# Taking the last pass over 64 contraction rows out of each product and running it as four 64-row matmuls per pair

## The chip, the core and the metric

The kernel runs on one core of one Trainium2 chip. The metric is the time of one execution on the device in microseconds (us); lower is better. The kernel before was timed in three runs: median 755.26 us, 754.84 to 755.68 us.

## What is computed

The reference mixes two branches with a gate. Only branch B is touched by the change; its core, with S = 2048 and D = 576, is:

```
a = einsum("bsd,ed->bse", x, dft_hid_re)        # x Wr
b = einsum("bsd,ed->bse", x, dft_hid_im)        # x Wi
y = einsum("ts,bse->bte", dft_seq_re, a) - einsum("ts,bse->bte", dft_seq_im, b)
return g * attention(x) + (1 - g) * y           # g = sigmoid(x . gate_w)
```

The products x Wr and x Wi contract over the 576 hidden columns: four chunks of 128 rows and a rest of 64 rows (`KC = 4`, `REST = 64`).

## The kernel before, in words

**Numbers.** Every fp32 operand is split into a high part (ScalarE copies it to the type fp32r, `hi_of`, line 112) and a low part (VectorE subtracts, `lo_of`, line 115). A product is high x high + high x low + low x high; low x low is dropped.

**One product.** `steps` (line 187) lists the matmuls of one 128-row tile of x with one half (288 columns) of a weight matrix: three for each of the four 128-row chunks, then two for the rest:

```
yield xs[:, 4], rhs(4)
yield xs[:, 9], rhs(4)
```

The 64 rest rows of x lie twice in the 128 partitions (`_rows` and `twice` on the host side), the high part in `xs[:, 4]` and the low part in `xs[:, 9]`. Row 4 of the weights, `hi[:, KC]` in `Wide.split` (line 241), holds the high part in partitions 0 to 63 and the low part in 64 to 127. The first of the two matmuls so adds high x high and high x low at once; the second adds low x high, and low x low with it. That makes 14 matmuls of 128 contraction rows, 128 stationary columns and 288 moving columns for one product (line 123 in the profile, through `run`).

**The order of the work.** The program goes through stages: features of k, k-v sums, q and the gate, the output matrix M and its product, then x Wr (`pairs(wdr, mr)`, line 779), the product with Cr (`sequence`, line 642), x Wi (`pairs(wdi, mi)`, line 782), the product with Ci. In `pairs` (line 542) 16 tiles of x are taken in 8 pairs (`NP = 8`); a pair is the four products of two tiles `i` with two column halves `h`. The six first pairs (`for p in range(NP - 2)`, line 574) do all four, tile by tile (pair 0 half by half), and the last two pairs are written apart (lines 589 to 603). After the second half of a tile its slot, one of three, is loaded with a later tile (`load_next`, line 171, a DMA of 320 KB on SyncE's queue) and an earlier loaded one is split (`split_next`). Each product has a PSUM bank, four to a pair, of eight. `columns` (line 552) reads the two banks of half 0 into the factors `f`, `rest` (line 560) reads all four into sums `tsum` and splits them.

**Who orders the queues.** The order on each engine is written before the run by a planner that replays the program against its own cost model (`schedule_with_timeline_sim=True`). SyncE's queue follows program order up to line 756 and the planner from there on. The planner may also move matmuls of one product ahead of those of another.

**What the change and the steps of the prediction touch:** `Wide.__init__` and `Wide.split` (lines 208 and 228), the loop of the six pairs (lines 574 to 582), `columns` and `rest`, and the two `Wide(...)` of Wr and Wi (lines 723 and 760).

Of the kernel before, what the change touches and what calls it, by code (L numbers as in the profile page):

```python
# [9 lines left out]
R = mybir.dt.float32r  # L10
AF = mybir.ActivationFunctionType
# [3 lines left out]
P = 128  # L15
S, D, H, DH = 2048, 576, 32, 18
NT = S // P
KC = 4
REST = D - KC * P
NG, GW = 5, 126  # L20
HALF = D // 2
CU = 4
NCU = NT // CU
NP = NT // 2
# [23 lines left out]
class Ring:  # L48
# [5 lines left out]
    def next(self):  # L54
# [5 lines left out]
TPAIR = 2 * 7 * HALF * 4  # L60
XD = 2 * D * 4
T_AT = 0
ACC_AT = T_AT + NP * TPAIR
SLOT_AT, SLOT = ACC_AT + NT * D * 4 + 256, 7 * BS * P * 4
# [8 lines left out]
LAY_R = dict(xs=(-256, 4864, 15744), hi=(20864, 9984), lo=(26624, 31232),  # L73
             low=(5, 3, 2, 1), high=(6, 0, 4))
LAY_I = dict(xs=(35840, 40960, 20096), hi=(25216, 14336), lo=(31232, 46080),
             low=(0, 4, 2, 3), high=(1, 5, 6))
# [3 lines left out]
def kernel(  # L80
# [14 lines left out]
    nc = tc.nc  # L95
# [4 lines left out]
    def at(offset, shape, dtype=F, name="t"):  # L100
        count[0] += 1
        t = nc.alloc_sbuf_tensor_at(f"{name}_{count[0]}", list(shape), dtype,
                                    offset=base + offset)
        return t.ap()
# [3 lines left out]
    def bank():  # L108
        return psum.tile([P, 512], F, tag="bank", name="bank")

    def hi_of(dst, src, bias=0.0):
        return nc.scalar.activation(dst, src, AF.Copy, bias=bias)  # L112

    def lo_of(dst, src, hi):
        nc.vector.tensor_tensor(out=dst, in0=src, in1=hi, op=ALU.subtract)  # L115

    def add(dst, a, b, op=ALU.add):
        nc.vector.tensor_tensor(out=dst, in0=a, in1=b, op=op)  # L118

    def run(ps, pairs):  # L120
        pairs = list(pairs)
        for n, (a, b) in enumerate(pairs):
            nc.tensor.matmul(ps, a, b, start=(n == 0), stop=(n == len(pairs) - 1))  # L123
# [47 lines left out]
    def load_next():  # L171
        if order:
            xs, raw = new_xs()
            nc.sync.dma_start(out=raw, in_=xa[order.pop(0)])
            raws.append((xs, raw))

    def split_next():
        if raws:
            xs, raw = raws.pop(0)
            hi_of(xs[:, 0:5], raw)  # L180
            lo_of(xs[:, 5:10], raw, xs[:, 0:5])
            split.append(xs)
# [4 lines left out]
    def steps(xs, rhs):  # L187

        for c in range(KC):
            yield xs[:, c], rhs(c)  # L190
            yield xs[:, c], rhs(5 + c)
            yield xs[:, 5 + c], rhs(c)
        yield xs[:, 4], rhs(4)
        yield xs[:, 9], rhs(4)
# [10 lines left out]
    class Wide:  # L205


        def __init__(self, src, lay, start=SLOT_AT, widths=(HALF, HALF)):
            self.src, self.lay, self.got = src, lay, {}
            self.start, self.widths = start, widths  # L210

        def load(self, h, pieces=1, queues=None):
            n = self.widths[h]
# [14 lines left out]
        def split(self, h, n=1):  # L228

            hi, los, rest = self.got[h]  # L230
            for c, lo, raw in los:
                k = lo.shape[1]
                m = max(k * n // KC, 1)
                for a in range(0, k, k // m):
                    cs = slice(a, a + k // m)
                    hs = slice(c + a, c + a + k // m)
                    hi_of(hi[:, hs], raw[:, cs])
                    lo_of(lo[:, cs], raw[:, cs], hi[:, hs])
                    yield
            hi_of(hi[:, KC], rest)  # L240
            lo_of(hi[64:, KC], rest[64:], hi[64:, KC])
            yield

        def row(self, h, j):
# [60 lines left out]
    xs = [First(), split.pop(0)]  # L305
# [34 lines left out]
    for i in range(2, NT):  # L340
        xs = split.pop(0)
# [56 lines left out]
    for c in range(5):  # L398
        ps = [bank(), bank()]
        passes = FULL if c < KC else FULL[:2]  # L400
        for q in range(NCU):
            t = xg_split.pop(0)
            for k in range(CU):
                s = q * CU + k
                for n, (a, b) in enumerate(passes):
                    for h in range(2):
                        nc.tensor.matmul(ps[h][:, :HALF], t[:, a, k], pk[s][:, b, half(h)],  # L407
                                         start=(s == 0 and n == 0),
                                         stop=(s == NT - 1 and n == len(passes) - 1))
# [132 lines left out]
    def pairs(wd, m):  # L542


        def product(b, i, h, xs):
            run(b[i][h], steps(xs[i], lambda j: wd.row(h, j)))

        def banks():
            b12, b11, b22, b21 = (bank()[:, :HALF] for _ in range(4))
            return (b11, b12), (b21, b22)  # L550

        def columns(p, b):

            t = at(T_AT + p * TPAIR, [P, 2, 7, HALF], R, "f")
            for i in range(2):
                hi_of(t[:, 0, i], b[i][0])
                lo_of(t[:, 1, i], b[i][0], t[:, 0, i])
            return t

        def rest(b, t):  # L560
            (b11, b12), (b21, b22) = b
            s = at(Y_AT, [P, 4, HALF], F, "tsum")
            nc.scalar.activation(s[:, 3], b12, AF.Copy)
            add(s[:, 0], s[:, 3], b11, ALU.subtract)
            add(s[:, 2], b22, s[:, 3], ALU.subtract)
            hi_of(t[:, 0, 2], b22)
            add(s[:, 1], b22, s[:, 0], ALU.subtract)
            add(s[:, 3], s[:, 1], b21, ALU.subtract)
            lo_of(t[:, 1, 2], b22, t[:, 0, 2])
            hi_of(t[:, 0, 3:7], s)  # L570
            lo_of(t[:, 1, 3:7], s, t[:, 0, 3:7])
            factors.append(t)

        for p in range(NP - 2):
            xs = [split.pop(0), split.pop(0)]
            b = banks()
            for i, h in sorted(((0, 0), (0, 1), (1, 0), (1, 1)), key=lambda u: u[not p]):
                product(b, i, h, xs)
                if h == 1:
                    load_next()  # L580
                    split_next()
            rest(b, columns(p, b))
            if p == NP - 4:
                m.load(0)
                m.make(0)
        xs_ring.at, xs_ring.n = [T_AT + NP * TPAIR - XS], 0
        load_next()
        split_next()
        last, p = [], NP - 2
        for k in range(2):  # L590
            xs, b = [split.pop(0), split.pop(0)], banks()
            for i in (0, 1) if k == 0 else (1, 0):
                product(b, i, 0, xs)
            if k == 0:
                split_next()
            last.append((b, xs, columns(p + k, b)))
        m.load(1)
        for b, xs, t in last:
            for i in range(2):
                product(b, i, 1, xs)  # L600
            if t is last[0][2]:
                m.make(1)
            rest(b, t)
# [103 lines left out]
    def transposed(i):  # L707

        xs, _ = new_xs("qs", qs_ring)
        banks = [bank(), bank()]  # L710
        twice = at(T_AT + 36864 + (i % 2) * 512, [P, 2, REST], F, "twice")
        nc.vector.tensor_copy(out=twice,
                              in_=acc[i][:, KC * P:].unsqueeze(1).to_broadcast([P, 2, REST]))
        for c in range(5):
            a = acc[i][:, c * P:(c + 1) * P] if c < KC else twice.rearrange("p a b -> p (a b)")
            nc.tensor.transpose(banks[c // KC][:, (c % KC) * P:(c % KC + 1) * P], a, ident)  # L716
        hi_of(xs[:, 0:4], banks[0])
        lo_of(xs[:, 5:9], banks[0], xs[:, 0:4])
        hi_of(xs[:, 4], banks[1][:, :P])
        lo_of(xs[:, 9], banks[1][:, :P], xs[:, 4])  # L720
        return xs

    wdr = Wide(wr, LAY_R)
    qs = transposed(0)
    for i in range(NT):
        if i + LEAD < NT:
# [30 lines left out]


    mr, mi = Matrix(cr, LAY_R), Matrix(ci, LAY_I)
    wdi = Wide(wi, LAY_I)  # L760

    def late(n):
        if n == NP * NB - 3:
# [75 lines left out]
```

## Time and profile before

| | |
|---|---|
| median of three runs | 755.26 us (754.84 to 755.68) |
| the profiled execution's own time | 754.51 us |
| its span, first to last instruction | 752.8 us |
| mean granted TensorE clock | 0.998 |
| TensorE matmul busy / weight load busy | 738.9 us / 736.3 us |
| VectorE busy / ScalarE busy | 543.1 us / 331.3 us |

The span is what one execution's trace shows; the time around it (1.7 us here) is outside every instruction. "PE" is TensorE's matmuls, "PEld" its weight loads, "DVE" VectorE, "ACT" ScalarE, "SP" SyncE. A matmul's recorded duration is longer than the distance to the next one's start, since matmuls are pipelined; what a matmul costs in a full stream is the distance of the starts.

### The profile page before, as it was taken

The numbers are of one execution on the slowest core, as the hardware profiler recorded it, in microseconds if no ns is written. First come the engines' busy times: TensorE is split into PE (matmuls) and PEld (weight loads), VectorE is DVE, ScalarE is ACT, GpSimd is POOL, SyncE is SP. The second block draws the span as 40 slices with busy tenths as digits, with TensorE's granted clock in tenths as the row PEclk, the third lists the DMA queues.
The fourth block names the chain that finished last, engine by engine and source line by source line (L and its number), as shares of the span: only waits on it lengthen the run. The fifth ranks groups of instructions, "written<-read, shape, count | busy, mean of one in ns | idle before, by whom it ended". The sixth has DMA issues, their size and how long they took to land.

```text
span 752.8 us, 13507 instructions
## 1 busy us (share of the span) xinstructions
PE 738.9 (98%) x5540; PEld 736.3 (98%) x5540; DVE 543.1 (72%) x915; ACT 331.3 (44%) x534; POOL 1.6 (0%) x10
## 2 busy tenths in 40 slices
PE   7999999997999999999999999999999999999998
PEld 7999999987999999999999999999999999999998
DVE  5668853757967228778888787778778887788784
ACT  6777334647546435544322323334554232322321
POOL 0000000000000000000000000000000000000000
PEclk9999999999999999999999999999999999999999
DMA  5334534152104013232323223234322243334331
GB/s 165 89 88 157 186 97 140 54 157 63 53 2 147 1 45 89 88 101 91 108 84 107 90 85 112 84 102 140 90 71 94 103 144 125 135 117 139 120 104 45
DMA packets 31641, 75.55 MB, mean 100 GB/s; under 512 B 3227, under 2 KB 8987, under 8 KB 31579
## 3 DMA queue, kind: packets, MB, share of 16 engines
q1 hardware_dynamic: 31291, 74.27, 30.9%
q8 instruction: 44, 0.72, 0.4%
q10 hardware_dynamic: 288, 0.41, 0.2%
q14 instruction: 18, 0.15, 0.1%
HBM read 68.47 MB, written 4.72 MB: 97 GB/s over the span
## 4 chain that ended last, share of the span: by engine, by line
PE 94%; DMA 3%; DVE 1%; issue 1%; ACT 0%; SPq 0%; ACTq 0%; DVEq 0%
PE bank L660 47%; PE bank L123 37%; PE bank L407 8%; DMA xraw<-in_xa_dram 3%; PE bank L716 1%; PE bank L392 1%; DMA wraw<-in_wr_dram 1%; DVE xs L115 0%; DVE wd L115 0%; SPq L507 0%; ACT xs L112 0%; ACT wd L112 0%; DVE acc L465 0%; DVE qs L115 0%; DVE acc L258 0%
## 5 line engine op out<-in xcount | busy, mean ns | idle before, releaser
L660 PE MATMUL bank<-f,c 128*128 128x288 f32 x2688 | 356.8, 295 | 0.0
L660 PEld LDWEIGHTS bank<-f,c 128*128 128x128 f32 x2688 | 356.6, 188 | 0.0
L123 PE MATMUL bank<-wd,xs 128*128 128x288 f32 (+1 forms) x1792 | 246.5, 299 | 10.1 <-ACT xs L112 5.2
L123 PEld LDWEIGHTS bank<-wd,xs 128*128 128x128 f32 x1792 | 242.5, 191 | 12.2 <-ACT xs L112 5.7
L112 ACT ACTIVATE c<-craw 128x1792 fp32r<-128x1792 f32 (+1 forms) x84 | 121.3, 1448 | 224.5 <-DVE craw L118 183.9
L115 DVE TENSOR_TENSOR c<-craw,c 128x1792 fp32r<-128x1792 f32 (+2 forms) x84 | 141.7, 1690 | 36.3 <-ACT c L112 36.1
L118 DVE TENSOR_TENSOR craw<-craw 128x256 f32<-128x256 f32 (+1 forms) x192 | 96.4, 509 | 51.8 <-DMA craw<-in_cr_dram 24.5
L115 DVE TENSOR_TENSOR xs<-xraw,xs 128x640 fp32r<-128x640 f32 (+1 forms) x65 | 52.5, 810 | 25.9 <-ACT xs L112 24.8
L123 PE MATMUL bank<-mw,qs 128*128 128x288 f32 x448 | 63.3, 298 | 0.6 <-DVE qs L115 0.6
L112 ACT ACTIVATE xs<-xraw 128x640 fp32r<-128x640 f32 x63 | 46.3, 737 | 38.5 <-DMA xraw<-in_xa_dram 38.3
L123 PEld LDWEIGHTS bank<-mw,qs 128*128 128x128 f32 x448 | 60.0, 188 | 0.8 <-DVE qs L115 0.8
L407 PE MATMUL bank<-pk,c 128*128 128x288 f32 x448 | 60.8, 296 | 0.0
L407 PEld LDWEIGHTS bank<-pk,c 128*128 128x128 f32 x448 | 59.8, 188 | 0.0
L118 DVE TENSOR_TENSOR y<-bank,y 128x288 f32<-128x288 f32 x63 | 28.6, 453 | 9.5 <-PE bank L660 8.8
L258 DVE SCALAR_TENSOR_TENSOR acc<-bank,e 128x288 f32<-128x288 f32 x64 | 27.8, 448 | 10.2 <-ACT e L257 10.1
L256 ACT ACTIVATE e<-bank 128x288 f32<-128x288 f32 x64 | 25.6, 401 | 18.0 <-PE bank L123 17.9
L115 DVE TENSOR_TENSOR f<-tsum,f 128x1152 fp32r<-128x1152 f32 x16 | 21.7, 1356 | 13.3 <-ACT f L112 13.3
L257 ACT ACTIVATE e<-e 128x288 f32<-128x288 f32 x64 | 28.0, 439 | 0.9
L735 ACT ACTIVATE acc<-bank,gate 128x288 f32<-128x288 f32 x32 | 16.0, 499 | 27.8 <-PE bank L123 27.5
L112 ACT ACTIVATE f<-bank 128x288 fp32r<-128x288 f32 x48 | 19.2, 401 | 20.2 <-PE bank L123 11.7
L115 DVE TENSOR_TENSOR f<-bank,f 128x288 fp32r<-128x288 f32 x48 | 21.4, 448 | 8.7 <-ACT f L112 8.7
L112 ACT ACTIVATE f<-tsum 128x1152 fp32r<-128x1152 f32 x16 | 18.6, 1163 | 17.4 <-DVE tsum L118 17.4
(67 smaller groups left out, 321.0 us busy)
## 6 DMA issues: line engine op xcount, KB each, us to landing
xraw<-in_xa_dram SPq DMA_DIRECT2D x63, 320.0 KB, 3.0
craw<-in_cr_dram SPq DMA_DIRECT2D x32, 512.0 KB, 3.3
craw<-in_ci_dram SPq DMA_DIRECT2D x32, 512.0 KB, 3.3
craw<-in_xg_dram SPq DMA_DIRECT2D x20, 256.0 KB, 3.2
out_dram<-acc SPq DMA_DIRECT2D x14, 288.0 KB, 3.2
wraw<-in_wv_dram SPq DMA_DIRECT2D x5, 288.0 KB
wraw<-in_wr_dram SPq DMA_DIRECT2D x2, 576.0 KB, 4.0
wraw<-in_wi_dram SPq DMA_DIRECT2D x2, 576.0 KB
```

The source lines that it names most:

```text
L112: return nc.scalar.activation(dst, src, AF.Copy, bias=bias)
L115: nc.vector.tensor_tensor(out=dst, in0=src, in1=hi, op=ALU.subtract)
L118: nc.vector.tensor_tensor(out=dst, in0=a, in1=b, op=op)
L123: nc.tensor.matmul(ps, a, b, start=(n == 0), stop=(n == len(pairs) - 1))
L256: nc.scalar.activation(e, ps, AF.Relu, scale=-1.0)
L257: nc.scalar.activation(e, e, AF.Exp, scale=-1.0)
L258: nc.vector.scalar_tensor_tensor(dst, ps, 0.0, e, op0=ALU.max, op1=ALU.add)
L392: nc.tensor.matmul(kv_of(g), wvt[c][:, a, gs], gts[c][:, :, gs], start=(c == 0 and a == 0 and g % 2 == 0), stop=(c == 4 and a == 1), skip_ ...
L407: nc.tensor.matmul(ps[h][:, :HALF], t[:, a, k], pk[s][:, b, half(h)], start=(s == 0 and n == 0), stop=(s == NT - 1 and n == len(passes) - 1))
L660: nc.tensor.matmul(ps[q], c[x][:, l, k], factors[p][:, y, f], start=(p == 0 and i == 0), stop=(p == NP - 1 and i == 2))
L716: nc.tensor.transpose(banks[c // KC][:, (c % KC) * P:(c % KC + 1) * P], a, ident)
L735: nc.scalar.activation(acc[i][:, half(h)], ps[:, :HALF], AF.Copy, scale=gate[:, i:i + 1])
```

## The change

It applies to the six first pairs of the Wr stage and of the Wi stage. The second of the two rest matmuls is taken out of each product. Instead the low rest `xs[i][:, 9]` of each tile is copied by ScalarE into a small buffer of its own (`ends`, four buffers of 512 bytes per partition in a ring, `lows`), and after the four products of a pair four matmuls of 64 contraction rows follow: for half 0 on partitions 0 to 63, for half 1 on 64 to 127. For this the weights' row 4 of half 1 is stored the other way round (`flip`: low part in 0 to 63, high part in 64 to 127). All four banks of a pair are so complete only at its end. Low x low of the rest is no longer added there. Everything else stays.

```diff
-            lo_of(hi[64:, KC], rest[64:], hi[64:, KC])
+            side = slice(0, REST) if self.flip and h == 1 else slice(REST, P)
+            lo_of(hi[side, KC], rest[side], hi[side, KC])
...
+        lows = Ring(T_AT + (NP - 1) * TPAIR, P * 4, 4)
         for p in range(NP - 2):
             xs = [split.pop(0), split.pop(0)]
-            b = banks()
+            b, ends = banks(), []
             for i, h in sorted(((0, 0), (0, 1), (1, 0), (1, 1)), key=lambda u: u[not p]):
-                product(b, i, h, xs)
+                if h == 0:
+                    ends.append(at(lows.next(), [P, P], R, "low"))
+                    nc.scalar.activation(ends[i], xs[i][:, 9], AF.Copy)
+                for n, (a, w) in enumerate(list(steps(xs[i], lambda j: wd.row(h, j)))[:-1]):
+                    nc.tensor.matmul(b[i][h], a, w, start=(n == 0), stop=False)
                 if h == 1:
                     load_next()
                     split_next()
+
+            for i in range(2):
+                for h in range(2):
+                    rows = slice(h * REST, (h + 1) * REST)
+                    nc.tensor.matmul(b[i][h], ends[i][rows], wd.row(h, KC)[rows],
+                                     start=False, stop=True)
             rest(b, columns(p, b))
...
-    wdr = Wide(wr, LAY_R)
+    wdr = Wide(wr, LAY_R, flip=True)
...
-    wdi = Wide(wi, LAY_I)
+    wdi = Wide(wi, LAY_I, flip=True)
```

## Rows read from the trace of the kernel before

**Rows 1.** The page: busy time of each engine, and the granted clock in 40 slices.

```profile
PE 738.9 (98%) x5540; PEld 736.3 (98%) x5540; DVE 543.1 (72%) x915; ACT 331.3 (44%) x534; POOL 1.6 (0%) x10
...
PEclk9999999999999999999999999999999999999999
```

**Rows 2.** The chain that ended last, in time: start us, length us, what, count.

```profile
267.01 66.76 PE bank L123 x504
...
512.04 59.34 PE bank L123 x448
```

**Rows 3.** What TensorE waited for in the whole run: us, times, longest us.

```profile
PE bank L123 <- ACT xs L112: 5.2, 2, 4.0
PE bank L123 <- DVE xs L115: 4.1, 2, 3.8
```

**Rows 4.** Groups with shapes apart, 274.4 to 333.7 us (Wr stage).

```profile
L123 PE MATMUL bank<-wd,xs 128*128 128x288 f32 x448 | 59.5, 295 | 0.0
...
L115 DVE TENSOR_TENSOR f<-bank,f 128x288 fp32r<-128x288 f32 x23 | 10.3, 449 | 8.5 <-ACT f L112 8.5
L115 DVE TENSOR_TENSOR xs<-xraw,xs 128x640 fp32r<-128x640 f32 x12 | 9.8, 820 | 2.6 <-ACT xs L112 2.5
...
L112 ACT ACTIVATE xs<-xraw 128x640 fp32r<-128x640 f32 x12 | 8.8, 737 | 4.9 <-DMA xraw<-in_xa_dram 4.9
L115 DVE TENSOR_TENSOR f<-tsum,f 128x1152 fp32r<-128x1152 f32 x6 | 8.1, 1358 | 7.4 <-ACT f L112 7.4
...
L118 DVE TENSOR_TENSOR tsum<-bank,tsum 128x288 f32<-128x288 f32 x14 | 6.3, 450 | 0.0
L118 DVE TENSOR_TENSOR tsum<-tsum,bank 128x288 f32<-128x288 f32 x14 | 6.2, 446 | 0.6 <-ACT tsum L563 0.6
...
L563 ACT ACTIVATE tsum<-bank 128x288 f32<-128x288 f32 x7 | 2.8, 406 | 2.6 <-DVE f L115 2.0 <-PE bank L123 0.6
```

**Rows 5.** Busy time by stretch: Wr stage, Wi stage, four pairs of each.

```profile
274.40:333.70 59.30, 59.30 (x450) 59.30 (x449) 41.41 (x76) 29.59 (x51) 0.00 (x0) 1.00 0.29 85
512.00:571.30 59.30, 59.30 (x450) 59.30 (x449) 45.95 (x83) 29.51 (x52) 0.00 (x0) 1.00 0.32 95
...
281.70:311.40 29.70, 29.70 (x227) 29.70 (x226) 22.37 (x40) 16.29 (x29) 0.00 (x0) 1.00 0.32 96
519.40:549.10 29.70, 29.70 (x227) 29.70 (x226) 22.43 (x39) 16.86 (x29) 0.00 (x0) 1.00 0.34 98
```

**Rows 6.** Timeline, where stationaries of 72 columns are followed by 128 columns.

```profile
87.74 0.14 PEld L392 LDWEIGHTS bank<-gt,plain 128*72 128x72 f32 x1
87.80 0.19 PEld L407 LDWEIGHTS bank<-pk,c 128*128 128x128 f32 x1
...
87.91 0.19 PEld L407 LDWEIGHTS bank<-pk,c 128*128 128x128 f32 x1
...
87.86 0.34 PE L407 MATMUL bank<-pk,c 128*128 128x288 f32 x1
...
88.04 0.42 PE L407 MATMUL bank<-pk,c 128*128 128x288 f32 x2
```

**Rows 7.** Timeline, single weight loads and matmuls around 300.3 us, Wr stage.

```profile
300.24 0.19 PEld L123 LDWEIGHTS bank<-wd,xs 128*128 128x128 f32 x1
...
300.24 0.42 PE L123 MATMUL bank<-wd,xs 128*128 128x288 f32 x2
```

**Rows 8.** Groups with shapes apart, whole run: the nearest small copy and low split.

```profile
L112 ACT ACTIVATE qs<-bank 128x128 fp32r<-128x128 f32 x16 | 4.4, 275 | 0.0
...
L115 DVE TENSOR_TENSOR wd<-wraw,wd 64x288 fp32r<-64x288 f32 x7 | 3.2, 455 | 0.7 <-ACT wd L112 0.6
```

**Rows 9.** The page, DMA issues: count, KB each, us to landing.

```profile
xraw<-in_xa_dram SPq DMA_DIRECT2D x63, 320.0 KB, 3.0
```

**Rows 10.** Timeline of VectorE after the sixth pair of the Wr stage.

```profile
323.99 0.44 DVE L118 TENSOR_TENSOR tsum<-tsum,bank 128x288 f32<-128x288 f32 x1
```

More of the change, by code (lines that the diff above doesn't have):

```diff
@@ L205, with __init__ @@
     class Wide:
-        def __init__(self, src, lay, start=SLOT_AT, widths=(HALF, HALF)):
+        def __init__(self, src, lay, start=SLOT_AT, widths=(HALF, HALF), flip=False):
             self.src, self.lay, self.got = src, lay, {}
-            self.start, self.widths = start, widths
+            self.start, self.widths, self.flip = start, widths, flip
         def load(self, h, pieces=1, queues=None):
```

## The prediction

> **What bounds the kernel now.** The page comes first: TensorE's matmuls and its weight loads are each busy for 98% of the span, VectorE for 72%, ScalarE for 44%, and the granted clock is at its upper level, 2.4 GHz, in all forty slices [rows 1]. Busy matmuls alone prove little, so the chain that ended last is read next. In the two touched stages it is one unbroken run of line 123: 448 matmuls in 59.34 us for Wi, and for Wr the last 448 of 504 in 66.76 us [rows 2]. Both give 132.5 ns from one matmul to the next. The list of TensorE's waits confirms it: the long ones are four, 9.3 us together, on tiles of x [rows 3], and neither touched stage has any, since its matmuls were preceded by 0.0 us of idle time [rows 4] and fill the whole window [rows 5]. So a matmul slot taken out of these stages shortens the run by 132.5 ns, as long as the others stay as dense, and work on VectorE or ScalarE costs nothing until TensorE has to wait for it.
>
> **What goes and what comes on TensorE.** A pair has 56 matmuls and takes 7.42 us. Four of them, 4 x 132.5 = 530 ns, become matmuls of 64 contraction rows with the same 288 moving columns. The count stays; a gain exists only if the two column halves, on different halves of the array and in different banks, run side by side. If they do, the four take two slots, 265 ns, and a pair gains 265 ns. Nothing in the trace has fewer than 72 contraction rows, so neither the overlap nor the change of form has a row. I bound both.
>
> *The change of form.* It comes twice per pair, into 64 rows and out again. From below I take 0. From above, everything in flight must end first: a matmul lasts 295 ns [rows 4] of which 132.5 are its slot, so 162 ns per change, and 108 ns more if the next weights can't be loaded meanwhile (two loads without cover start 87.80 and 87.91 us, [rows 6]; in a stream the load of the next weights starts with the matmul before, both at 300.24, [rows 7]). The nearest row is where the stationary's shape changes in mid stream: the first 128-column matmul after two of 72 columns starts at 87.86 and the next at 88.04, a step of 0.18 us instead of 0.1325 [rows 6]. That is 45 ns over, and I take it for each change: 90 ns per pair.
>
> *The sum.* 265 - 90 = 175 ns per pair; six pairs in two stages make 12, so 2.1 us less. Bounds with overlap: 265 x 12 = 3.2 us less; with a full flush 530 - 265 - 325 = -60 ns per pair, 0.7 us more; with flush and bare loads (265 - 2 x 270 = -275 ns) 3.3 us more. Without overlap and with flush and bare loads it is 540 ns per pair, 6.5 us more.
>
> The Trainium skill, page "TensorE: Matmul & The Clock Gate", section "Part 3: Packing small matmuls", says that matmuls in different row groups run concurrently, with starts some 4 ns apart. By that alone the sum would be the 3.2 us; no run so far shows it.
>
> **The rest, costed at nothing, with its cover.** *The copies.* 24 copies of 128 x 128 on ScalarE, some 275 ns each (the nearest row reads PSUM, [rows 8]), 6.6 us in all, 0.55 us per pair. ScalarE is busy 16.3 to 16.9 us of 29.7 in four pairs [rows 5], about 4.2 of 7.42 us. A copy waits for the tile's low part; queued behind it are the high parts of the banks and of the next tile, and for these VectorE waits. But a tile is split before its pair needs it, so the wait is short. If ScalarE's cover were gone, each copy would delay the split of one tile by its 0.28 us. *The flipped low part* is the same VectorE instruction on the other 64 partitions, 455 ns [rows 8]. *SyncE and POOL.* No DMA is added, and none is moved past another in program order; the load of a later tile follows 26 instead of 28 matmuls of its slot's old tile, a quarter us earlier, and also needs the copy. A load lands after 3.0 us [rows 9], then 0.74 and 0.82 us of split [rows 4]: 4.6 us, against the 7.2 us until the tile freed at a pair's end is replaced by one that is needed a whole pair later. Spare: 2.6 us less queueing. *The banks.* Before, the two banks of half 0 could be read while the pair ran; now all reads start at its end. VectorE has 3 x 449 + 2 x 450 + 2 x 446 ns = 3.1 us of them, after a copy of 0.41 us on ScalarE; with both tile splits (1.6 us) and the last split of the sums (1.36 us) in between, 6.5 us [rows 4]. The banks are wanted again one pair, 7.2 us, later. It fits: VectorE's load per pair stays 5.6 of 7.2 us [rows 5]. The tight place is after the sixth pair: in program order the first product of the eighth pair takes its banks back 28 matmuls, 3.7 us, later. The sixth pair ended near 267.01 + 7.42 + 6 x 7.42 = 318.9 us, and its last bank was read until 324.4 [rows 10], 5.5 us on, without a pause on TensorE, since other products can go ahead. Two more reads (0.9 us) now stand behind the end, so 6.4 us. I take 0; the upper end is 6.4 - 3.7 = 2.7 us per stage.
>
> **The rivals.**
>
> *Weight loads in single file (754.1).* Overlapping matmuls need two weight loads per 132.5 ns. Where nothing covers them loads start 108 ns apart, 87.80 and 87.91 us [rows 6]. If loads for the two halves can't overlap either, the four matmuls take 4 x 108 = 432 ns instead of 530: 98 ns per pair, 1.2 us in all. For it: the load of 72 columns takes 0.14 us against 0.19 for 128 [rows 6], so columns set its time, and the columns stay 128. Against it: no row shows two loads for different rows. The Trainium skill, same page, section "LDWEIGHTS (loading the stationary operand)", says so outright: columns count, and a load of 32 rows takes as long as one of 128. The trace agrees on columns and shows nothing on rows.
>
> *No overlap (755.3).* The change doesn't do what it says: four slots stay four slots, and the changes of form are free.
>
> *A flush at each change, with overlap (756.0).* The -60 ns per pair above: no measurable difference.
>
> *A flush with a bare load behind it (758.6), the slower side.* Both changes of form cost 162 + 108 = 270 ns. The whole change turns slower by 0.2% where one change of form costs over (265 + 1510/12)/2 = 195 ns. For it: a matmul's 295 ns against its slot of 132.5 show how much is in flight. Against: TensorE goes from 72 to 128 stationary columns for 45 ns [rows 6]. The Trainium skill, page "TensorEngine Tiling (Array Packing)", section "Key Properties", has this rule: a change of the tiling mode drains TensorE. It speaks against the change and gives no length; no row before shows it, as all loads are of one mode's kind. By it the time is one of these last two.
>
> *TensorE waits for banks or tiles (about 757).* Gain 2.1 us, loss 2.7 to 5.4 us at the sixth pair of both stages: 755.9 to 758.6.
>
> **The numbers.** Forecast, overlap with a small price: 0.40, 1.5 to 3.2 us less. Single file 0.19, no overlap 0.06, flush with overlap 0.10: these three are "same", 0.35. Flush with bare load 0.17, waits 0.08: "slower", 0.25. The bound of 0.2%, 1.5 us, is about what a measurement can tell from no change; the three runs of before spread over 0.84 us. The sum was made on an execution of 754.51 us (span 752.8 us), 0.75 below the median; differences are applied to the median: 755.26 - 2.1 = 753.2. The range runs from the full gain less 0.2 us of spread, 751.9, to 757.6, which leaves out the bare-load flush and a fifth of the waits: 0.19.
>
> **What would show it.** Right: in the Wr and Wi stages the 64-row matmuls of the two halves start within some tens of ns of each other, the first full matmul after them starts about 350 ns after the first of the four would have started, and each stage is 1.0 us shorter in the chain (58.3 us). Single file: four starts 108 ns apart. No overlap: 132.5 apart. A flush: a step of 295 ns or more into the first 64-row matmul and again behind the last. Waits: idle time of TensorE put down to line 115 or 118 near the sixth pair. What would make the forecast wrong is above all a change of form dearer than 70 ns (then the gain falls under 1.5 us), or halves that don't start together.

## The result, and the profile after

The changed kernel takes 758.59 us (757.8 to 758.9) beside 755.05 us of the kernel before: 1.0047 times, 95% interval 1.0034 to 1.006. It is slower by 0.47%, 3.5 us. The profiled execution has a span of 757.0 us. The forecast was 753.2 us in a range of 751.9 to 757.6; the result lies on the other side, above the range.

First the page's busy time of each engine, then, from the groups with shapes apart, the two of line 592 (the 64-row matmuls):

```profile
PE 744.1 (98%) x5540; PEld 736.1 (97%) x5540; DVE 543.7 (72%) x915; ACT 336.4 (44%) x558; POOL 1.6 (0%) x10
...
L592 PE MATMUL bank<-wd,low 64*128 64x288 f32 x48 | 8.1, 358 | 0.0
L592 PEld LDWEIGHTS bank<-wd,low 64*128 64x128 f32 x48 | 4.3, 184 | 2.8 <-issue 2.5 <-ACT xs L112 0.3
```

The count of matmuls is 5540 as before, and TensorE is busy 5.2 us longer [rows 1]. Weight loads were never idle in these stages; now 2.8 us of idle time stand right before the 64-row loads. The chain that ended last, in time (start us, length us, what, count), for the first pairs of the Wr stage and the last stretch of each stage:

```profile
274.65 6.89 PE bank L584 x52
...
282.00 3.64 PE bank L584 x26
285.64 0.33 PE bank L592 x2
285.97 4.18 PE bank L584 x30
...
290.48 6.57 PE bank L584 x48
...
336.11 178.30 PE bank L672 x1344
514.41 3.70 PE bank L584 x28
518.11 0.46 PE bank L592 x2
...
575.66 178.12 PE bank L672 x1344
```

The unbroken runs of before [rows 2] are cut into pieces, and many pieces aren't the 52 full matmuls of one pair. From its first matmul to that of the next stage Wr takes 336.11 - 274.65 = 61.5 us and Wi 575.66 - 514.41 = 61.3 us, where each took 59.3 to 59.4 before. That is 2.1 and 1.9 us more. The two profiled spans differ by 4.2 us (757.0 and 752.8) and the medians by 3.5, so nearly the whole loss is in the two touched stages.

TensorE's weight loads waited as follows (us, times, longest us):

```profile
PEld bank L592 <- issue: 2.5, 15, 0.2
PEld bank L592 <- ACT xs L112: 0.3, 2, 0.2
```

15 + 2 = 17 waits of some 0.17 us, each before the first load of a group of 64-row matmuls. The change writes 12 groups of four. The planner made 17 of them: seven of four, one of three, eight of two and a lone one. The pieces of 26 and 30 in the chain are its cuts. Two of the groups of two, in the first pair of Wi, hold the same column half of both tiles. They don't overlap: the chain gives such a group 0.46 us (at 518.11) and a group of two different halves 0.33 (at 285.64).

One group of four, in the Wi stage, by narrow windows of the timeline (a row with x2 or x4 starts with the first of them):

```profile
544.74 0.29 PE L584 MATMUL bank<-wd,xs 128*128 128x288 f32 x1
...
544.96 0.19 PEld L592 LDWEIGHTS bank<-wd,low 64*128 64x128 f32 x2 [0.16 <-issue]
544.96 0.40 PE L592 MATMUL bank<-wd,low 64*128 64x288 f32 x2
...
544.96 0.30 PEld L592 LDWEIGHTS bank<-wd,low 64*128 64x128 f32 x4 [0.16 <-issue]
544.96 0.53 PE L592 MATMUL bank<-wd,low 64*128 64x288 f32 x4
...
545.20 0.29 PE L592 MATMUL bank<-wd,low 64*128 64x288 f32 x2
...
545.42 0.30 PEld L584 LDWEIGHTS bank<-wd,xs 128*128 128x128 f32 x2 [0.16 <-issue]
545.42 0.40 PE L584 MATMUL bank<-wd,xs 128*128 128x288 f32 x1
```

Read it from the top. The last full matmul starts at 544.74. In a stream the next load would start with it [rows 7]; here the first loads of the new form start at 544.96, 0.22 us later. Both loads of the two halves start together, and so do their matmuls (two such matmuls, one per half, are a duo), which last 0.40 us instead of 0.29: they wait 0.11 us for their own weights, which nothing hid. The second two start together at 545.20, without such a wait. Then the same again: 0.22 us to the load for full matmuls (545.42), and a first full matmul of 0.40 us. So the halves do run side by side, four matmuls in two slots. But a change of form, from 128-row to 64-row matmuls or back, costs 0.22 + 0.11 us in place of a slot of 0.1325, some 197 ns, twice per group: a group of four loses 2 x 197 - 265 = 129 ns, one duo 261 ns, a lone matmul 394 ns. 17 groups cost 34 changes x 197 = 6.7 us, and 21 of 24 possible overlaps give back 21 x 132.5 = 2.8 us: 3.9 us net, against 4.0 us in the stages.

### The profile page after: what moved, and what is told of

The parts are those of the page before. It is cut to its first block, busy times and chain, and to the rows that moved or that the text cites. A ratio compares the mean times of both kernels' runs of the same rounds, so it can differ in the third digit from the quotient of the medians.

```text
span 757.0 us, 13540 instructions
## 1 busy us (share of the span) xinstructions
PE 744.1 (98%) x5540; PEld 736.1 (97%) x5540; DVE 543.7 (72%) x915; ACT 336.4 (44%) x558; POOL 1.6 (0%) x10
## 4 chain that ended last, share of the span: by engine, by line
PE 94%; DMA 3%; DVE 1%; issue 1%; ACT 0%; ACTq 0%; DVEq 0%; SPq 0%
PE bank L672 47%; PE bank L123 25%; PE bank L584 11%; PE bank L408 8%; DMA xraw<-in_xa_dram 3%; PE bank L592 1%; PE bank L728 1%; PE bank L393 1%; DMA wraw<-in_wr_dram 1%; DVE wd L115 0%; DVE xs L115 0%; ACT xs L112 0%; ACT wd L112 0%; DVE qs L115 0%; DVE acc L466 0%
## 5 line engine op out<-in xcount | busy, mean ns | idle before, releaser
L123 PE MATMUL bank<-wd,xs 128*128 128x288 f32 (+1 forms) x1120 | 159.0, 303 | 9.4 <-ACT xs L112 4.7
L123 PEld LDWEIGHTS bank<-wd,xs 128*128 128x128 f32 x1120 | 154.8, 194 | 11.7 <-ACT xs L112 5.5
L584 PE MATMUL bank<-wd,xs 128*128 128x288 f32 x624 | 87.1, 297 | 0.0
L584 PEld LDWEIGHTS bank<-wd,xs 128*128 128x128 f32 x624 | 83.3, 188 | 2.3 <-issue 1.0
```

Source lines behind the costliest of these rows:

```text
L584: nc.tensor.matmul(b[i][h], a, w, start=(n == 0), stop=False)
```

## The experiments

All compare with runs of the kernel before on the same chip (754.3 to 754.7 us there).

**Full rows at the end.** Place, copies and late banks as in the change, without the 64-row form and without the flipped low part.

```diff
-                    rows = slice(h * REST, (h + 1) * REST)
-                    nc.tensor.matmul(b[i][h], ends[i][rows], wd.row(h, KC)[rows],
+                    nc.tensor.matmul(b[i][h], ends[i], wd.row(h, KC),
                                      start=False, stop=True)
...
-    wdr = Wide(wr, LAY_R, flip=True)
+    wdr = Wide(wr, LAY_R)
...
-    wdi = Wide(wi, LAY_I, flip=True)
+    wdi = Wide(wi, LAY_I)
```

> The change with its copies, its place at the end of the pair and its late banks, but the four last matmuls on all 128 rows (no 64-row form, nothing flipped). Theory (each change between 128-row and 64-row matmuls costs some 197 ns, nothing else matters): 755.1 us, as before, within 0.4. Rival (the loss comes from copies, late banks or tiles, whatever the form of the matmuls): 758 to 759, with idle time of TensorE at the sixth pair.

Measured 755.59 us beside 754.59: 1.0014 times (1.0005 to 1.0023), 1.0 us more. Neither value was quite met: moving costs a little, far less than the 3.5 us. The planner cut these matmuls into the same 17 groups, in the same order, as in the changed kernel, so the form of the matmuls (with the flip, which it needs) is all that differs. What TensorE's loads waited for, and the place (timeline, 524.3 to 525.4 us):

```profile
PEld bank L584 <- DVE xs L115: 0.5, 1, 0.5
...
524.18 1.55 DVE L115 TENSOR_TENSOR xs<-xraw,xs 128x640 fp32r<-128x640 f32 x2
...
525.05 0.43 PEld L584 LDWEIGHTS bank<-wd,xs 128*128 128x128 f32 x3 [0.52 <-DVE xs L115]
```

One tile of x comes 0.5 us late in the second pair of Wi, when VectorE has two tiles to split at once; the sixth pair, which I had feared, shows nothing.

**Four together.** The 64-row matmuls are pinned, so that the planner can't part them (this is "the pinned kernel" below).

```diff
-                    nc.tensor.matmul(b[i][h], ends[i][rows], wd.row(h, KC)[rows],
-                                     start=False, stop=True)
+                    tc.keep_in_program_order(nc.tensor.matmul(
+                        b[i][h], ends[i][rows], wd.row(h, KC)[rows], start=False, stop=True))
```

> The change with its four 64-row matmuls pinned behind the pair's last full matmul, so that they stay together: 12 groups in place of the 17 of the changed kernel. Theory (price per change of form): a group of four costs 2 x 197 - 265 = 130 ns, 12 x 130 = 1.6 us over before: 756.6, 2.0 us under the changed kernel. Rival (the place or the banks): 758.6, as the changed kernel, since those are the same.

Measured 756.72 us: 1.0028 times (1.0017 to 1.004), 2.1 us more than before, where the change itself cost 3.5. Twelve groups, as the count of waits shows, and the one late tile again (0.6 us):

```profile
PEld bank L592 <- issue: 2.0, 12, 0.2
...
PEld bank L584 <- DVE xs L115: 0.6, 1, 0.6
```

12 x 129 ns = 1.5 us plus 0.6 make the 2.1. Without the planner's cuts the loss so is 1.4 us smaller. The changed kernel's own list of waits has no late tile there, so by count the cuts cost more than this difference (2.4 us, see below). Why the planner cuts wasn't tried.

**One half.** As the pinned kernel, both column halves on partitions 0 to 63.

```diff
-                    rows = slice(h * REST, (h + 1) * REST)
+                    rows = slice(0, REST)
...
-    wdr = Wide(wr, LAY_R, flip=True)
+    wdr = Wide(wr, LAY_R)
...
-    wdi = Wide(wi, LAY_I, flip=True)
+    wdi = Wide(wi, LAY_I)
```

> As the pinned kernel, but both column halves on partitions 0 to 63 (nothing flipped): the same matmuls, all on one half of the array. Theory (halves overlap when they lie on different halves of the array): 132.5 ns more for each of 24 duos, 3.2 us: 759.8. Rival (no gain by overlap): 756.6, as pinned.

Measured 759.41 us: 1.0064 times (1.005 to 1.0079), 2.7 us over the pinned kernel. The overlap is real and worth what two slots per pair are worth, less 0.5 us. The timeline of one group, and its first load by a narrow window with the two behind it:

```profile
305.42 0.79 PE L592 MATMUL bank<-wd,low 64*128 64x288 f32 x4
...
305.42 0.18 PEld L592 LDWEIGHTS bank<-wd,low 64*128 64x128 f32 x1 [0.16 <-issue]
...
305.53 0.32 PEld L592 LDWEIGHTS bank<-wd,low 64*128 64x128 f32 x2
```

From the first start to the last end, four matmuls take 0.79 us here and 0.53 in the changed kernel. On one half the second load starts 0.11 us after the first, on two halves with it: loads for the two halves are not in single file.

**Twelve together.** As the pinned kernel, one full matmul of each product left out, the group three times over.

```diff
+                    if n == 3 * KC - 1:
+                        continue
...
+            for n in range(3):
+                for i in range(2):
+                    for h in range(2):
...
```

> As the pinned kernel, but one full matmul of each product (low x high of the fourth chunk) is left out and the group of four 64-row matmuls runs three times in a row, so that rest low x high counts three times: 4 slots go, 8 half slots come. Theory (price per change of form, not per matmul): 756.6, as pinned. Rival (each 64-row matmul pays some 100 ns, by its weight load): 12 x (12 x 99 - 265) = 11 us more than before: 766.

Measured 755.64 us: 1.0014 times (1.0005 to 1.0024), 1.0 us more than before (0.4 to 1.8) and a little below the expected 756.6. The rival's 766 is out: the price is paid per change of form, not per 64-row matmul. There are 144 of these matmuls and still 12 waits:

```profile
PEld bank L595 <- issue: 2.0, 12, 0.2
...
L595 PE MATMUL bank<-wd,low 64*128 64x288 f32 x144 | 12.7, 308 | 0.0
```

**Two per tile.** The two matmuls of a tile behind its own products, without copies.

```diff
-                if h == 0:
-                    ends.append(at(lows.next(), [P, P], R, "low"))
-                    nc.scalar.activation(ends[i], xs[i][:, 9], AF.Copy)
...
+                    for e in range(2):
+                        rows = slice(e * REST, (e + 1) * REST)
+                        tc.keep_in_program_order(nc.tensor.matmul(
+                            b[i][e], xs[i][rows, 9], wd.row(e, KC)[rows], start=False, stop=True))
```

> The two 64-row matmuls of a tile right behind its products, straight from the tile: no copies and no bank later than its tile's end, but 24 groups of two. Theory: 24 x (2 x 197 - 132.5) = 24 x 262 ns = 6.3 us: 761.4. Rival (copies and late banks are the loss): 755 or less.

Measured 760.86 us: 1.0081 times (1.0066 to 1.0097), 6.1 us more, as expected. No copy is made and no bank is kept open past its tile, and yet it is slower than the change itself, as 24 round trips into the 64-row form and back would have it.

**64 rows in place, 96 rows in place.** The kernel before, with only the last pass of each product cut.

```diff
-            run(b[i][h], steps(xs[i], lambda j: wd.row(h, j)))
+            todo = list(steps(xs[i], lambda j: wd.row(h, j)))
+            a, w = todo.pop()
+            run(b[i][h], todo + [(a[:64], w[:64])])
```

> The kernel before with the last pass of each of the 64 products of the two stages cut to rows 0 to 63 in its place (only low x low is left out): nothing moved, copied or overlapped. Theory: 64 lone matmuls, each between two changes of form, 64 x 395 ns = 25 us: 780. Rival (64-row matmuls cost no more than others): 755.1.

> The same, cut to 96 rows instead of 64 (half of low x low is left out). Theory (the price is for the change to matmuls that take half the array, not for fewer active rows): 755.1, as before. Rival (every matmul on part of the rows pays): 780, as with 64.

With 64 rows 779.87 us: 1.0336 times (1.0317 to 1.0354), 25.1 us more. With 96 rows 754.96 us: 1.0 (0.9989 to 1.001). From the groups of each:

```profile
L123 PE MATMUL bank<-wd,xs 64*128 64x288 f32 x64 | 25.3, 395 | 0.0
```

```profile
L123 PE MATMUL bank<-wd,xs 96*128 96x288 f32 x64 | 19.0, 297 | 0.0
```

64 lone matmuls at 394 ns make 25.2 us. This is the cleanest pair: nothing moves, the rows alone are cut, and the price appears with 64 rows and not with 96. The trace of the kernel before narrows it further. It has six matmuls of 72 rows among others of 126 and 128 rows, and they last 295 ns like those, where a lone one of 64 rows lasts 395:

```profile
L123 PE MATMUL bank<-plain,kvb 72*72 72x288 f32 x6 | 1.1, 295 | 0.0
```

Their starts, and those of the matmuls behind them, follow each other in 0.13 to 0.14 us (147.6 to 151.4 us). So the price sets in between 72 and 64 rows.

**A short matmul before the change of form.** As pinned, the last full matmul and the second duo cut to half their columns.

```diff
+                    c = HALF // 2 if (i, h) == (1, 1) and n == 3 * KC else HALF
...
+                        b[i][h][:, :HALF // (1 + i)], ends[i][rows],
+                        wd.row(h, KC)[rows][:, :HALF // (1 + i)], start=False, stop=True))
```

> As the pinned kernel, with the last full matmul of a pair and the second duo of its group cut to 144 of 288 columns (the other columns leave this pass out). For the trace: in the changed kernel the first weight load of the other form starts 223 ns after the start of the last matmul of the old form, 120 ns of it for the moving columns. Theory (TensorE lets the old form run empty before it loads for the new): the distance falls by 60 ns, to 163, on both sides. Rival (a fixed time of switching): it stays 223.

One execution (755.72 us), run for its trace alone. Narrow windows of the timeline around its first group:

```profile
280.98 0.23 PE L585 MATMUL bank<-wd,xs 128*128 128x144 f32 x1
...
281.14 0.19 PEld L595 LDWEIGHTS bank<-wd,low 64*128 64x128 f32 x2
...
281.38 0.23 PE L595 MATMUL bank<-wd,low 64*128 64x144 f32 x2
...
281.53 0.19 PEld L585 LDWEIGHTS bank<-wd,xs 128*128 128x128 f32 x1
```

From the start of the short matmul to the loads it is 0.16 us instead of 0.22, and on the way back, from the short duo at 281.38 to the load at 281.53, the same. The distance shrinks with the last matmul of the old form, so it is not a fixed time of switching. This is what one expects if TensorE runs empty before it loads for the other form. The Trainium skill, page "TensorEngine Tiling (Array Packing)", section "Key Properties", says that a change of the tiling mode drains TensorE; this trace agrees, with 0.16 us behind a matmul of 144 columns and 0.22 behind one of 288.

**Eight together.** Two pairs' ends in one group, all eight banks open.

```diff
+        for o in range(0, NP - 2, 2):
+            held = []
+            for p in (o, o + 1):
...
+                held.append((p, b, ends))
+            for p, b, ends in held:
+                for i in range(2):
+                    for h in range(2):
...
+            for p, b, ends in held:
+                rest(b, columns(p, b))
+            if p == NP - 3:
```

> The 64-row matmuls of two pairs in one group of eight, six groups in all: all eight banks stay open until the group. Theory: a change of form pays here (2 x 197 - 4 x 132.5 = -136 ns a group, 0.8 us in all), but the next pair's first product has no free bank until ScalarE has copied one or two banks (0.4 us each) and VectorE has read them twice (0.9 us): some 1.3 us of waiting at each of six groups, 8 us: about 762. Rival (the planner finds cover for the banks): 754.3, faster than before.

Measured 772.35 us: 1.0235 times (1.0212 to 1.0257), 18 us more, over twice the expected loss. What TensorE's loads waited for:

```profile
PEld bank L586 <- ACT tsum L564: 7.4, 8, 1.4
...
PEld bank L677 <- ACT c L112: 4.9, 4, 1.6
...
PEld bank L677 <- DVE c L115: 4.0, 4, 1.3
```

In the pairs the banks come late in eight places, not six, and the 7.4 us there are near the 8 that I expected. The rest is mainly in the next stage (line 677), which waits 8.9 us for its first matrices; this I hadn't seen. It may be that the queues that read the banks fall behind, but the edit also moves the first load and split of those matrices (`m.load(0)`, `m.make(0)`) from behind the fifth pair to behind the sixth, and the two weren't told apart. By count a larger group pays for its changes of form; here it loses far more on waits. No version tried here is faster than the kernel before.

## Why the prediction was wrong

**The bound** was right: the stages are TensorE's alone, and of the 4.2 us between the two profiled spans 4.0 were lost there. Only its reading of the clock was too even. At 172 to 181 us, behind a wait of 11.7 us for a tile, the granted clock is partly at its lower level, 1.2 GHz: its mean is 0.81 in the kernel before and 0.62 in the changed one. In the touched stages it is 1.00 in both, so nothing here hangs on it.

**Overlap** was right. The halves start together and four matmuls take two slots; one half instead of two costs 2.7 us.

**The price of a change of form** is the step that failed. I put it at 45 ns, by the row that I called the nearest, where the stationary goes from 72 to 128 columns [rows 6]. That row shows an unhidden part of a weight load: the first 128-column matmul there lasts 0.34 us instead of 0.295, and no load comes 0.22 us late. Where the trace of before goes from 126 to 72 rows and columns and on to 128, in a stream of 288 moving columns, there is no such step at all (0.13 to 0.14 us from start to start). So the row was near in looks alone. Measured: 197 ns, made of the run empty (0.22 us from the last start to the load) and a bare load (0.11 us), less a slot. My own upper row had both parts, 162 + 108 = 270 ns; it counted the run empty from a full matmul's modelled duration, 295 ns, which is longer than the 0.22 us after which the loads start. For the same reason the sign that I gave for a flush, a step of 295 ns or more, isn't in the trace: it is 0.22 us to the recorded start, and the other 0.11 us lie inside the first matmul's 0.40. The point I gave from which the change turns slower by 0.2%, 195 ns, was met almost exactly, which is why the pinned kernel ends about there.

**Twelve groups** was the second step that failed: I took the program's four for the order on the queue, though I had noted that the planner may move matmuls ahead of others. It made five groups more, each for another 394 ns, and lost three overlaps. The price alone turns the gain of 2.1 us into a loss of 1.5, about 756.8 us; the extra groups bring the result above the range. The "flush with bare load" rival gave 758.6 and the result is 758.59, but that is luck, for its terms are others: 24 changes at 270 ns, where there were 34 at 197.

**The covers** held nearly. Copies (0.31 us each), SyncE's loads and the late banks together cost 1.0 us (0.4 to 1.7) with full rows at the end, 0.5 us of it at one late tile in the Wi stage; I had put 0 there, and feared the sixth pair, where there is nothing. In the changed kernel itself that wait is absent, and the changes of form account for 3.9 of the stages' 4.0 us. The flipped low part, which that run doesn't have, takes 452 ns instead of 455 [rows 8].

**Single file** fell: the two loads start together.

With the measured price the sum reads: 12 pairs x (2 x 197 - 265) = 1.5 us slower, plus five more round trips and three lost overlaps, 5 x 394 + 3 x 132.5 = 2.4 us: 3.9 us in the stages.

## What to carry to other kernels

A small matmul that shares the array pays only if the work it saves exceeds what TensorE loses by running empty and reloading, here 394 ns per round trip, three slots of 288 columns. Four half-array matmuls so lose; six should break even, which is an estimate from the 197 and 132.5 ns, as no run here shows a gain. Price a change of form as "run empty plus one bare load" (a load that no earlier matmul hides), never by a row where the form stays the same. And where a planner writes the order, look at how many groups it really makes, since each costs a round trip.

## What was unexpected in the hardware

Matmuls of 96 rows leave the time as it was (1.0, 0.9989 to 1.001), and those of 72 rows in the trace of before last as long as full ones, but 64 rows cost 394 ns when alone. So it is not every missing row that costs, but the step to half the array. And once in the 64-row form, two halves keep pace without loss: twelve in a row cost no more waiting than four, with both weight loads of a duo hidden behind the duo before.
